# Two quads' inverse norms finished on VectorE, and a reordered opening, in a cosine-attention and feed-forward kernel

## The chip, the cores and the metric

The kernel runs on one core of a Trainium2 chip. The metric is the device time of one execution in microseconds (us); several runs are taken and the median is used. A profiled execution gives a trace: each instruction of each engine with its start, its duration and what ended the wait ahead of it. The engines are PE (matrix products), PEld (PE's weight loads, which overlap them), ACT (activation functions), DVE (elementwise work, reductions, copies), POOL (elementwise work, and a DMA queue of its own) and SP (a DMA queue).

## What is computed

```python
def _attn_ref(q, k, v, tau):                     # (8, 12, 448, 64)
    q_n = q / (np.linalg.norm(q, axis=-1, keepdims=True) + 1e-06)
    k_n = k / (np.linalg.norm(k, axis=-1, keepdims=True) + 1e-06)
    scores = np.matmul(q_n, k_n.transpose(0, 1, 3, 2)) / tau
...
    attn = np.exp(scores)                        # less the row's largest
    attn = attn / (np.sum(attn, axis=-1, keepdims=True) + 1e-09)
    return np.matmul(attn, v).astype(np.float32)

def _moe_ref(x, w_in, w_out):                    # (3584, 768), (768, 2048), (2048, 768)
    h = x @ w_in
    g = h * np.cos(h)
    return (g @ w_out).astype(np.float32)
```

The attention output, with its heads side by side, is the x of the second part.

## The kernel before

Work is cut into 24 "quads", numbered from 0. A quad is four heads of one batch row, three quads to a row. A quad's 448 keys are seven blocks of 64, so the score steps are numbered g = 7 * quad + j. A step's scores go to one of two pairs of PSUM banks (0 and 1, or 2 and 3), ACT takes their exponential into a tile E (one of 17), and PE uses E twice: in `attend` (E times V, into banks X and Y, 4 and 5) and in a sum over the keys. At the end of a quad, the AV product is multiplied by the inverse of the sums into xT, the input of the second part.

Before that, each quad is normalized. `square` takes squares of Qf and Kf, DVE adds them up into n2 (line 445), `inverse` (lines 452 to 470) turns n2 into 1 / (norm + 1e-6) by four ACT instructions, Ln, Exp, Ln, Exp, each waiting for the one before, and `scale` (472) writes Qn and Kn. Then Qn and Kn are transposed to qT and kT.

The first three quads (FIRST = 3) are the opening, lines 782 to 842. Their order on ACT, DVE and POOL is the order in which the program states them (`P.strict`), as it is on PE in the whole kernel. In the opening the transposes are PE matmuls against an identity (`transpose`, 493) with a DVE copy out of PSUM, the sums are `spread` (563, matmuls against ones, into banks 6 and 7, called Z) followed by Ln and Exp of the sums on ACT into ar (581, 582), and `scale_x` (585) multiplies banks X and Y by ar on DVE. `stir` (590) adds products with zeros to Z and `warm` (737) multiplies the identity with itself; both only keep PE occupied.

After the opening comes, for each batch row: `m1` (x times W1, then h cos h by two ACT and two DVE instructions for each pair of blocks, lines 642 to 668), `m2` (g times W2, 670 to 691, evicted by DVE copies to osb at line 684), and the scores of the next quads between the m2 parts. Quads 3 and later are scaled on POOL and transposed by DMAs from SP's queue (`turn`, 512). The normalization of quads 3 and 4 (lines 845 and 848) waits for the last ACT instruction of the opening.

Loads: Q and K of a quad are two DMAs of 448 KB on SP's queue (`load_one`), V and the weights are DMAs on POOL's queue. The load of quad 5's Q and K (line 799, `load_qk(qd + 4, half[2])`) waits for the first two of the four W2 loads.

The order on ACT, DVE, POOL and SP behind the opening, and on SP everywhere, comes from the planner (lines 22 to 195). It plays the program through with costs written at each instruction, for DMAs with a model of two queues that slow each other (`land`, 70 to 81). On each engine it takes the instruction that can start first (line 157), unless another one that can start while that one would run is more urgent by more than its lateness, its cost and WORTH = 1.0 us (line 161); urgency is counted back from PE's program order. The emitted queues run in that order whatever the chip does.

```python
c = min(pending[e], key=lambda i: (max(now, ready_at[i]), ops[i].prio))
...
if su < s + ops[c].dur and ops[c].prio - ops[u].prio > su - s + ops[u].dur + self.WORTH:
```

Of the kernel before, what the change touches and what calls it, by code (L numbers as in the profile page):

```python
# [21 lines left out]
class Planner:  # L22
# [10 lines left out]
    FIRST, LAST = 1.2, 0.8  # L33
# [9 lines left out]
    def op(self, eng, dur, fn, r=(), w=(), after=(), dma=None, moves=0, mode="f", chain=None, keep=False, lead=0.0):  # L43
        o = Op()
        o.i, o.eng, o.dur, o.fn, o.dma, o.moves, o.mode, o.chain = (
            len(self.ops), eng, dur, fn, dma, moves, mode, chain)
        o.lat = self.FIRST + moves + self.LAST if dma else self.LAT[eng]
        o.behind, o.lead = None, lead
        if keep or self.strict and eng in ("act", "dve", "pool"):
            o.behind, self.tail[eng] = self.tail.get(eng), o  # L50
        o.reads, o.writes = tuple(r), tuple(w)
        deps = {a.i for a in after if a is not None}
        for x in o.reads:
            if x in self.last_write:
# [12 lines left out]
        self.ops.append(o)  # L67
        return o
# [203 lines left out]
def bass_cosine_attention__then__act_gcu_kernel(  # L272
# [12 lines left out]
    NJ = S // D  # L285
# [6 lines left out]
    FIRST = 3  # L292
# [5 lines left out]
    def sb(name, shape, dt):  # L298
        return ctx.enter_context(nc.sbuf_tensor(name, shape, dt))

    def ring(name, n, shape, dt):
        return [sb("%s%d" % (name, i), shape, dt) for i in range(n)]

    NE, NV, NA = 17, 4, 4
# [6 lines left out]
    sqq = sb("sqq", [128, 2 * NJ, D], BF16)  # L311
    sqk = sb("sqk", [128, 2 * NJ, D], BF16)
    n2 = ring("n2", 2, [128, 4 * NJ], F32)
    nrm = ring("nrm", 2, [128, 4 * NJ], F32)
    rr = ring("rr", 2, [128, 4 * NJ], F32)
    Qn = ring("Qn", 2, [128, NJ, 2, D], BF16)
    Kn = ring("Kn", 2, [128, NJ, 2, D], BF16)
# [10 lines left out]
    ident = sb("ident", [128, 128], BF16)  # L328
    sel = sb("sel", [128, 32], BF16)
    ones = sb("ones", [128, D], BF16)  # L330
    zeros = sb("zeros", [128, 128], BF16)
    PS = ctx.enter_context(nc.psum_tensor("PS", [128, 8 * 512], F32))
    rscr = nc.dram_tensor("rscr", [2 * B * 8, S], F32)

    def bank(i, n=S, p0=0, p1=128):
        return PS.ap()[p0:p1, 512 * i:512 * i + n]
# [5 lines left out]
    op = P.op  # L342
# [11 lines left out]
    op("dve", 0.3, fill_sel, w=["sel"])  # L354
    op("dve", 0.1, lambda e: e.memset(ones.ap(), 1.0), w=["ones"])

    op("dve", 0.1, lambda e: e.memset(zeros.ap(), 0.0), w=["zeros"])

    mode = [None]

# [8 lines left out]
    def act(m, dur, fn, r=(), w=(), **kw):  # L369
        table(m)  # L370
        return op("act", dur, fn, r=[*r, "table"], w=w, **kw)
# [6 lines left out]
    def cut(kind, u, part):  # L378

        return [(kind, u, i) for i, (j0, j1) in enumerate(HALVES) if part[0] < j1 and j0 < part[1]]  # L380
# [39 lines left out]
        return pool_dma(0.79, lambda e: e.dma_start(W2.ap()[:, 4 * i:4 * i + 4, :], src),  # L420
                 w=[("W2", i)], dma=("W2", i), moves=4.32, after=after)

    H, NLEAD = 2 * NJ, 5.0

    def jr(t, w, part, off=0):
        return bass.AP(t, off + w * H + part[0], [[2 * H, 128], [NJ, 2], [1, part[1] - part[0]]])
# [24 lines left out]

    def inverse(qd, w0, w1, part=ALL[0], after=()):

        u = qd % 2
        ws = range(w0, w1)
        x = [c for w in ws for c in cut("nrm%d" % w, u, part)]
        y = [c for w in ws for c in cut("rr%d" % w, u, part)]
        if part == ALL[0]:
            n = slice(H * w0, H * w1)
            t, z, o = n2[u].ap()[:, n], nrm[u].ap()[:, n], rr[u].ap()[:, n]  # L460
        else:
            t, z, o = (jr(a[u], w0, part) for a in (n2, nrm, rr))
        act("exp", 0.12, lambda e: e.activation(z, t, ACT.Ln, bias=1e-30, scale=1.0),
            r=[c for w in ws for c in cut("n2%d" % w, u, part)], w=x, after=after, lead=NLEAD * (qd > FIRST + 1))
        yield
        act("exp", 0.12, lambda e: e.activation(z, z, ACT.Exp, bias=0.0, scale=0.5), r=x, w=x, lead=NLEAD * (qd > FIRST + 1))
        yield
        act("exp", 0.12, lambda e: e.activation(z, z, ACT.Ln, bias=1e-6, scale=1.0), r=x, w=x, lead=NLEAD * (qd > FIRST + 1))
        yield
        act("exp", 0.12, lambda e: e.activation(o, z, ACT.Exp, bias=0.0, scale=-1.0), r=x, w=y, lead=NLEAD * (qd > FIRST + 1))  # L470

    def scale(qd, w, eng="pool", part=ALL[0]):
        s, u = qd % 3, qd % 2
# [50 lines left out]
    def scores(g):  # L524
        qd, j = divmod(g, NJ)
        assert holds.get(g % NE, 0) // NJ in summed or g < NE
        holds[g % NE] = g
        u, bs, es = qd % 2, 2 * (g % 2), g % NE

        def mm(e):  # L530
            for r in range(2):
                for a in range(2):
                    ins = e.matmul(bank(bs + r, S, 64 * a, 64 * a + 64),  # L533
                                   kT[u].ap()[64 * r:64 * r + 64, j, a, :],
                                   qT[u].ap()[64 * r:64 * r + 64, :, a, :],
                                   start=True, stop=True)
# [48 lines left out]
    def scale_x(qd):  # L585
        b, c0, s = qd // QB, 2 * (qd % QB), qd % 3
        op("dve", 1.01, lambda e: e.tensor_tensor(xT[b % 2].ap()[:, c0:c0 + 2, :], two(X), ar[s].ap(), ALU.mult),
           r=pair(X) + [("ar", s)], w=[("x", b % 2, qd % QB)])

    def stir(qd, n):  # L590

        g = NJ * qd

        def mm(e):
            for i in range(n):
                ins = e.matmul(bank(Z + i % 2), zeros.ap(), E[g % NE].ap()[:, i % 2, :], start=False, stop=False)
            return ins

        op("pe", 0.19 * n, mm, r=[("E", g % NE), "zeros"], w=pair(Z), mode="q")
# [182 lines left out]
    for qd in range(FIRST):  # L782
        g = NJ * qd
        for j in range(NJ):
            scores(g + j)
            if j == 1 and qd:
                spread(qd - 1, NJ - 2, NJ - 1)
                for i in range(2):
                    attend(g - NJ + i)
                stir(qd - 1, 1)  # L790
            if j == 1 and qd == 0:
                adds[1]()
                transpose(0, 1, 7, HALVES[1])
                warm(5, X)
            if j == 2 and qd == 0:
                warm(7, X)
            if j == min(qd, 1) + 1 and qd + 1 < FIRST:
                scaled = norm_b(qd + 1, "dve")
                load_qk(qd + 4, half[2] if qd else ())
            if j == 2 and qd:  # L800
                attend(g - NJ + 2)
                spread(qd - 1, NJ - 1, NJ)
            if j == 3 and qd:
                for i in range(3, NJ):
                    attend(g - NJ + i)
                load_v(qd - 1 + NV)
                scale_x(qd - 1)
                if qd + 1 == FIRST:
                    for x in squares:
                        x()  # L810
            if j == 2:
                squares = [square(qd + 2, w, "pool", after=[scaled]) for w in range(2)]
                if qd == 0:
                    load_v(3)
                    half[2] += [load_w2(f, ()) for f in range(2)]
                    half[3] += [load_w2(f, ()) for f in range(2, 4)]
            if j == (4 if qd else 3):
                spread(qd, 0, 2)
                stir(qd, 3)
            if j == 4:  # L820
                spread(qd, 2, 3)
                if qd == 0:
                    stir(qd, 2)
            if j == 5 and qd:
                stir(qd, 1)
            if j == 5 and qd + 1 < FIRST:
                transpose(qd + 1, 0, X)
            if j == 6:
                if qd + 1 < FIRST:
                    transpose(qd + 1, 1, Y)  # L830
                    for x in squares:
                        x()
                spread(qd, 3, 5)
                stir(qd, 1)
    for i in range(4):
        attend(g + i)
    spread(qd, NJ - 2, NJ - 1)
    for i in range(4, NJ):
        attend(g + i)
    load_v(qd + NV)  # L840
    spread(qd, NJ - 1, NJ)
    scale_x(qd)
    P.strict = False
    ended = [o for o in P.ops if o.eng == "act"]
# [107 lines left out]
```

## Time and profile before

| what | value |
|---|---|
| median of 3 runs | 447.37 us (446.12 to 447.99) |
| the profiled execution | 445.76 us, of which the span from first to last instruction is 444.0 us |
| PE busy | 421.2 us, 95% of the span |
| ACT busy | 315.2 us, 71% |
| DVE busy | 249.3 us, 56% |
| POOL busy | 209.1 us, 47% |
| PE busy in the opening, 0 to 36.4 us | 7.46 of 10.7, 6.77 of 7.3, 7.66 of 9.1, 8.60 of 9.3 us |
| PE busy behind it, 101 to 365 us | 258.8 of 264 us |

PE's busy time counts matmuls that overlap, with modelled ends, so a share near 100% says that PE hardly waits, not that it runs at its peak. The last row is the sum of five stages of the trace.

### The profile page before, as it was taken

The numbers are of one execution on the slowest core, as the hardware profiler recorded it, in microseconds if no ns is written. First come the engines' busy times: TensorE is split into PE (matmuls) and PEld (weight loads), VectorE is DVE, ScalarE is ACT, GpSimd is POOL, SyncE is SP. The second block draws the span as 40 slices with busy tenths as digits, with TensorE's granted clock in tenths as the row PEclk, the third lists the DMA queues.
The fourth block names the chain that finished last, engine by engine and source line by source line (L and its number), as shares of the span: only waits on it lengthen the run. The fifth ranks groups of instructions, "written<-read, shape, count | busy, mean of one in ns | idle before, by whom it ended". The sixth has DMA issues, their size and how long they took to land.

```text
span 444.0 us, 8347 instructions
## 1 busy us (share of the span) xinstructions
PE 421.2 (95%) x3527; PEld 205.2 (46%) x3527; DVE 249.3 (56%) x278; ACT 315.2 (71%) x449; POOL 209.1 (47%) x144
## 2 busy tenths in 40 slices
PE   7889978889999999989999999999999999999996
PEld 6334433334544345434454444434454445555553
DVE  5664963446873449723984239823583136825931
ACT  6998778897778767888678656878678666815700
POOL 4675159779169792478365564188033030030000
PEclk9999999999999999999999999999999999999999
DMA  8999996998618996169923795068801611051022
GB/s 272 253 235 210 180 300 135 211 260 183 188 52 181 261 210 193 35 139 250 218 71 79 197 215 174 1 159 186 180 2 36 161 39 38 0 156 35 1 71 71
DMA packets 70589, 64.79 MB, mean 146 GB/s; under 512 B 41924, under 2 KB 62744, under 8 KB 70552
## 3 DMA queue, kind: packets, MB, share of 16 engines
q1 hardware_dynamic: 60144, 52.31, 47.3%
q0 software_dynamic: 10240, 11.80, 16.4%
q8 instruction: 27, 0.44, 0.4%
q10 hardware_dynamic: 168, 0.15, 0.1%
q14 instruction: 10, 0.08, 0.1%
HBM read 55.25 MB, written 11.16 MB: 150 GB/s over the span
## 4 chain that ended last, share of the span: by engine, by line
PE 64%; ACT 11%; DMA 9%; POOL 6%; DVE 5%; issue 2%; SPq 1%; ACTq 1%; POOLq 0%
PE PS L648 25%; PE PS L676 24%; ACT E L540 8%; PE PS L533 6%; PE PS L550 4%; DMA Qf<-in_q_dram 3%; PE PS L615 3%; DMA Kf<-in_k_dram 3%; DMA kT<-Kn 2%; DVE n L445 1%; POOL xT L634 1%; POOL sqq L441 1%; POOL Kn L478 1%; POOL Qn L478 1%; POOL sqk L441 1%
## 5 line engine op out<-in xcount | busy, mean ns | idle before, releaser
L540 ACT ACTIVATE E<-PS 128x896 bf16<-128x896 f32 x168 | 145.3, 916 | 33.1 <-PE PS L533 28.4
L676 PE MATMUL PS<-W,gT 128*128 128x384 bf16 x896 | 163.4, 327 | 3.5 <-DVE osb L684 2.6
L648 PE MATMUL PS<-xT,W 128*128 128x448 bf16 x768 | 148.2, 353 | 0.9 <-DVE gT L667 0.8
L676 PEld LDWEIGHTS PS<-W,gT 128*128 128x128 bf16 x896 | 80.1, 98 | 83.9 <-issue 28.8
L648 PEld LDWEIGHTS PS<-xT,W 128*128 128x128 bf16 x768 | 74.1, 98 | 72.2 <-DVE gT L667 2.2
L661 ACT ACTIVATE ar<-PS 128x896 int32<-128x896 f32 x64 | 58.1, 910 | 45.6 <-PE PS L648 45.2
L663 DVE SCALAR_TENSOR_TENSOR ar<-ar,PS 128x896 f32<-128x896 int32 x64 | 69.0, 1083 | 26.3 <-ACT ar L661 26.3
L684 DVE COPY osb<-PS 128x384 f32<-128x384 f32 x56 | 30.3, 556 | 94.6 <-PE PS L676 94.6
L634 POOL TENSOR_TENSOR xT<-AVs,R 128x896 bf16<-128x896 f32 x21 | 43.6, 2085 | 71.5 <-DMA R<-rscr 71.3
L665 ACT ACTIVATE ar<-ar 128x896 f32<-128x896 f32 x64 | 60.6, 947 | 14.7 <-DVE ar L663 14.4
L667 DVE TENSOR_TENSOR gT<-PS,ar 128x896 bf16<-128x896 f32 x64 | 69.4, 1088 | 1.5 <-ACT ar L665 1.0
L533 PE MATMUL PS<-qT,kT 64*64 64x448 bf16 x672 | 55.3, 366 | 9.9 <-ACT E L540 7.6
L441 POOL TENSOR_TENSOR sqq<-Qf 128x896 bf16<-128x896 f32 x22 | 36.9, 1676 | 57.0 <-DVE n L445 26.6
L550 PE MATMUL PS<-E,Vb 64*64 64x448 bf16 x672 | 48.0, 351 | 0.3 <-DVE AVs L559 0.2
L478 POOL TENSOR_TENSOR Qn<-Qf,rr 128x896 bf16<-128x896 f32 x21 | 35.4, 1688 | 27.1 <-ACT rr L470 27.1
L441 POOL TENSOR_TENSOR sqk<-Kf 128x896 bf16<-128x896 f32 x22 | 36.9, 1677 | 21.5 <-DVE n L445 14.5
L559 DVE COPY AVs<-PS 128x896 f32<-128x896 f32 x21 | 22.9, 1090 | 27.2 <-PE PS L550 27.1
L533 PEld LDWEIGHTS PS<-qT,kT 64*64 64x64 bf16 x672 | 15.3, 104 | 45.9 <-ACT E L540 25.6
L445 DVE TENSOR_REDUCE n<-sqq 128x14 f32<-128x896 bf16 x24 | 25.9, 1081 | 17.1 <-POOL sqq L441 11.8
L478 POOL TENSOR_TENSOR Kn<-Kf,rr 128x896 bf16<-128x896 f32 x21 | 35.5, 1689 | 0.0
L445 DVE TENSOR_REDUCE n<-sqk 128x14 f32<-128x896 bf16 (+2 forms) x25 | 26.0, 1043 | 12.8 <-POOL sqk L441 12.7
L550 PEld LDWEIGHTS PS<-E,Vb 64*64 64x64 bf16 x672 | 19.5, 106 | 11.9 <-issue 2.4
(43 smaller groups left out, 163.2 us busy)
## 6 DMA issues: line engine op xcount, KB each, us to landing
Qf<-in_q_dram SPq DMA_DIRECT2D x24, 448.0 KB, 4.7
out_dram<-osb SPq DMA_DIRECT2D x56, 192.0 KB, 2.8
Kf<-in_k_dram SPq DMA_DIRECT2D x23, 448.0 KB, 5.7
R<-rscr SPq DMA_DIRECT2D x42, 224.0 KB, 4.5
Vb<-in_v_dram POOLq DMA_DIRECT2D x24, 224.0 KB, 7.0
W<-in_moe_w_in_dram POOLq DMA_DIRECT2D x4, 768.0 KB, 18.4
W<-in_moe_w_out_dram POOLq DMA_DIRECT2D x4, 768.0 KB, 24.9
qT<-Qn SPq DMA_TRANSPOSE x21, 4.6
```

The lines of the kernel that those rows point to most:

```text
L441: op(eng, (1.68 if eng == "pool" else 1.05) * n, lambda e: e.tensor_tensor(dst, src, src, ALU.mult), r=cut(nm + "f", s, part), w=cut("sq" ...
L445: return op("dve", 0.07 + 0.95 * n, lambda e: e.tensor_reduce(out=n2[u].ap()[:, H * w:H * w + H] if part == ALL[0] else jr(n2[u], w, part) ...
L478: lambda e: e.tensor_tensor(n[u].ap()[:, j0:j1].rearrange("p j r d -> p r j d"), f[s].ap()[:, :, j0:j1], rb, ALU.mult),
L533: ins = e.matmul(bank(bs + r, S, 64 * a, 64 * a + 64), kT[u].ap()[64 * r:64 * r + 64, j, a, :], qT[u].ap()[64 * r:64 * r + 64, :, a, :], s ...
L540: act("exp", 0.875, lambda e: e.activation(E[es].ap(), two(bs), ACT.Exp, bias=0.0, scale=INV_TAU), r=pair(bs), w=[("E", es)], chain="E")
L550: ins = e.matmul(bank((X, Y)[a], S, 64 * r, 64 * r + 64), Vb[vs].ap()[64 * a:64 * a + 64, r, j, :], E[es].ap()[64 * a:64 * a + 64, r, :], ...
L648: ins = e.matmul(bank(bk + i2), W1.ap()[:, i, 128 * nb:128 * nb + 128], xT[c % 2].ap()[:, i, :], start=(i == 0), stop=(i == NKC - 1))
L661: op("act", 0.815, lambda e: e.activation(ar[s].ap().bitcast(I32), two(bk), ACT.Identity, bias=0.25, scale=INV2PI), r=bs, w=[("ar", s)])
L663: op("dve", 1.005, lambda e: e.scalar_tensor_tensor(ar[s].ap(), ar[s].ap().bitcast(I32), -2.0 * math.pi, two(bk), ALU.mult, ALU.add), r=bs ...
L665: act("sin", 0.86, lambda e: e.activation(ar[s].ap(), ar[s].ap(), ACT.Sin, bias=GUARD * math.pi / 2.0, scale=GUARD), r=[("ar", s)], w=[("a ...
L667: op("dve", 1.01, lambda e: e.tensor_tensor(gT.ap()[:, 2 * pr:2 * pr + 2, col:col + S], two(bk), ar[s].ap(), ALU.mult), r=bs + [("ar", s)] ...
L676: ins = e.matmul(bank(bk, HW), gT.ap()[:, f, col:col + 128], W2.ap()[:, f, HW * h:HW * h + HW], start=(f == 0), stop=(f == NNB - 1))
```

## The change

Five things change; the names are those of the code.

1. `inverse` of quads 1 and 2 keeps Ln and Exp on ACT, which leave the norms. nrm becomes a tile of pairs: Exp writes one of a pair, the other holds 1e-6 from the start (`fill_eps`). A DVE reduction adds each pair, a DVE reciprocal follows. Quad 0 and quads 3 and later keep the four ACT instructions, on the wider nrm.
2. Quad 2 is transposed into Z and Z + 1 (banks 6 and 7) instead of X and Y. Quad 1's first sums, which used Z at that time, move to steps 0 and 1 of quad 2; quad 1's three `stir` calls of its own pass go, and `warm(8, Z)` stands ahead of the transposes. `scale_x(0)` moves behind the copies of those transposes.
3. In quad 0, the last two `spread` products are split around the transposes of quad 1, with one more `stir` product.
4. At the end of the opening the last `spread` stands ahead of the last three `attend` steps instead of behind them.
5. `zeros` shares the memory of `iot`, which is filled again once the identity is made.

```diff
-    nrm = ring("nrm", 2, [128, 4 * NJ], F32)
+    nrm = ring("nrm", 2, [128, 4 * NJ, 2], F32)
...
-    zeros = sb("zeros", [128, 128], BF16)
+    zeros = iot.ap().bitcast(BF16)[:, 0:128]
...
+    def fill_eps(e):
+        e.memset(nrm[0].ap(), 1e-6)
+        return e.memset(nrm[1].ap(), 1e-6)
...
+        if 0 < qd <= FAST:
+            op("dve", 0.13, lambda e: e.tensor_reduce(out=o, in_=both, axis=AX.X, op=ALU.add), r=cells("nrm") + ["eps"],
+               w=cells("rr"), lead=lead)
+            yield
+            op("dve", 0.27, lambda e: e.reciprocal(o, o), r=cells("rr"), w=cells("rr"), lead=lead)
+            return
...
             scores(g + j)
+            if j < 2 and qd == 2:
+                spread(qd - 1, 3 * j, 3 * j + 3 - j)
...
-                scale_x(qd - 1)
                 if qd + 1 == FIRST:
+                    scale_x(qd - 1)
...
-            if j == (4 if qd else 3):
+            if j == (4 if qd else 3) and qd != 1:
                 spread(qd, 0, 2)
                 stir(qd, 3)
             if j == 4:
-                spread(qd, 2, 3)
+                if qd == 1:
+                    warm(8, Z)
+                    transpose(qd + 1, 0, Z)
+                else:
+                    spread(qd, 2, 3)
...
-            if j == 5 and qd:
-                stir(qd, 1)
-            if j == 5 and qd + 1 < FIRST:
-                transpose(qd + 1, 0, X)
+            if j == 5:
+                if qd == 0:
+                    transpose(qd + 1, 0, X)
+                    spread(qd, 3, 4)
+                elif qd == 1:
+                    transpose(qd + 1, 1, Z + 1)
+                    scale_x(qd - 1)
+                else:
+                    stir(qd, 1)
...
-    for i in range(4):
+    for i in range(3):
         attend(g + i)
     spread(qd, NJ - 2, NJ - 1)
+    attend(g + 3)
+    spread(qd, NJ - 1, NJ)
     for i in range(4, NJ):
         attend(g + i)
     load_v(qd + NV)
-    spread(qd, NJ - 1, NJ)
     scale_x(qd)
```

More of the change, by code (lines that the diff above doesn't have):

```diff
@@ L355, in bass_cosine_attention__then__act_gcu_kernel @@
     op("dve", 0.1, lambda e: e.memset(ones.ap(), 1.0), w=["ones"])
-    op("dve", 0.1, lambda e: e.memset(zeros.ap(), 0.0), w=["zeros"])
+    op("dve", 0.1, lambda e: e.memset(zeros, 0.0), w=["zeros", "iot"])
+    def fill_eps(e):
+        e.memset(nrm[0].ap(), 1e-6)
+        return e.memset(nrm[1].ap(), 1e-6)
+    op("dve", 0.2, fill_eps, w=["eps"] + [(n, u, i) for n in ("nrm0", "nrm1") for u in range(2) for i in range(3)])
     mode = [None]
@@ L421, in load_w2 @@
                  w=[("W2", i)], dma=("W2", i), moves=4.32, after=after)
-    H, NLEAD = 2 * NJ, 5.0
+    H, NLEAD, FAST = 2 * NJ, 5.0, 2
     def jr(t, w, part, off=0):
@@ L455, in inverse, with cells @@
         ws = range(w0, w1)
-        x = [c for w in ws for c in cut("nrm%d" % w, u, part)]
-        y = [c for w in ws for c in cut("rr%d" % w, u, part)]
+        def cells(name):
+            return [c for w in ws for c in cut("%s%d" % (name, w), u, part)]
+        j0, j1 = part
+        rows = [NJ, 2 * (w1 - w0)], [1, j1 - j0]
         if part == ALL[0]:
[L459 to L462, printed above, removed]
@@ L463, in inverse @@
-        act("exp", 0.12, lambda e: e.activation(z, t, ACT.Ln, bias=1e-30, scale=1.0),
-            r=[c for w in ws for c in cut("n2%d" % w, u, part)], w=x, after=after, lead=NLEAD * (qd > FIRST + 1))
+            rows = [[1, H * (w1 - w0)]]
+        t, o = (bass.AP(x[u], w0 * H + j0, [[2 * H, 128], *rows]) for x in (n2, rr))
+        wide = [[2 * a, b] for a, b in rows]
+        z = bass.AP(nrm[u], 2 * (w0 * H + j0), [[4 * H, 128], *wide])
+        both = bass.AP(nrm[u], 2 * (w0 * H + j0), [[4 * H, 128], *wide, [1, 2]])
@@ L465, in inverse @@
+        lead = NLEAD * (qd > FIRST + 1)
+        act("exp", 0.12, lambda e: e.activation(z, t, ACT.Ln, bias=1e-30, scale=1.0), r=cells("n2"), w=cells("nrm"),
+            after=after, lead=lead)
         yield
-        act("exp", 0.12, lambda e: e.activation(z, z, ACT.Exp, bias=0.0, scale=0.5), r=x, w=x, lead=NLEAD * (qd > FIRST + 1))
+        act("exp", 0.12, lambda e: e.activation(z, z, ACT.Exp, bias=0.0, scale=0.5), r=cells("nrm"), w=cells("nrm"), lead=lead)
         yield
-        act("exp", 0.12, lambda e: e.activation(z, z, ACT.Ln, bias=1e-6, scale=1.0), r=x, w=x, lead=NLEAD * (qd > FIRST + 1))
+        if 0 < qd <= FAST:
[4 more added lines that the diff above has]
+            return
@@ L469, in inverse @@
+        act("exp", 0.12, lambda e: e.activation(z, z, ACT.Ln, bias=1e-6, scale=1.0), r=cells("nrm"), w=cells("nrm"), lead=lead)
         yield
-        act("exp", 0.12, lambda e: e.activation(o, z, ACT.Exp, bias=0.0, scale=-1.0), r=x, w=y, lead=NLEAD * (qd > FIRST + 1))
+        act("exp", 0.12, lambda e: e.activation(o, z, ACT.Exp, bias=0.0, scale=-1.0), r=cells("nrm"), w=cells("rr"), lead=lead)
     def scale(qd, w, eng="pool", part=ALL[0]):
@@ L595, in mm @@
             for i in range(n):
-                ins = e.matmul(bank(Z + i % 2), zeros.ap(), E[g % NE].ap()[:, i % 2, :], start=False, stop=False)
+                ins = e.matmul(bank(Z + i % 2), zeros, E[g % NE].ap()[:, i % 2, :], start=False, stop=False)
             return ins
@@ L820, in bass_cosine_attention__then__act_gcu_kernel @@
             if j == 4:
-                spread(qd, 2, 3)
+                if qd == 1:
[3 more added lines that the diff above has]
+                    spread(qd, 2, 3)
                 if qd == 0:
                     stir(qd, 2)
-            if j == 5 and qd:
-                stir(qd, 1)
-            if j == 5 and qd + 1 < FIRST:
-                transpose(qd + 1, 0, X)
-            if j == 6:
+            if j == 5:
[7 more added lines that the diff above has]
+                    stir(qd, 1)
+            if j == 6:
+                if qd == 0:
+                    transpose(qd + 1, 1, Y)
+                    spread(qd, 4, 5)
+                    stir(qd, 2)
+                elif qd == 2:
+                    spread(qd, 3, 5)
+                    stir(qd, 1)
                 if qd + 1 < FIRST:
-                    transpose(qd + 1, 1, Y)
                     for x in squares:
                         x()
-                spread(qd, 3, 5)
-                stir(qd, 1)
-    for i in range(4):
+    for i in range(3):
         attend(g + i)
     spread(qd, NJ - 2, NJ - 1)
+    attend(g + 3)
+    spread(qd, NJ - 1, NJ)
     for i in range(4, NJ):
```

## The prediction

> **What bounds the kernel now.** I read the busy time by stage first: behind 101 us PE is busy 258.8 of 264 us, so whatever shift arrives there goes through to the end, and whatever the change is worth is decided ahead of it. Next the chain that ended last, in order of time (start, us, what), where it leaves the opening:
>
> ```profile
> 37.45 0.96 ACT ar L582
> ...
> 39.52 1.68 POOL Qn L478
> 41.20 1.65 POOL Kn L478
> 42.85 1.65 POOL Qn L478
> 44.49 1.66 POOL Kn L478
> 46.15 2.27 SPq L517
> ...
> 48.54 11.07 DMA Qf<-in_q_dram
> ...
> 59.68 1.68 POOL sqq L441
> 61.36 1.65 POOL sqk L441
> ...
> 63.03 1.10 DVE n L445
> ...
> 64.15 0.23 ACT nrm L463
> ```
>
> The chain does not run through m1, which fills PE from 36.4 to 55 us. It runs through a load that takes 11.07 us: Q of quad 5. Its squares are added by DVE at 63.03, and what stands behind that addition is shown by the timelines of DVE and PE:
>
> ```profile
> 63.03 1.09 DVE L445 TENSOR_REDUCE n<-sqk 128x14 f32<-128x896 bf16 x1 [0.55 <-POOL sqk L441]
> 64.03 1.01 DVE L684 COPY osb<-PS 128x384 f32<-128x384 f32 x2
> 64.64 0.82 PE L676 MATMUL PS<-W,gT 128*128 128x384 bf16 x4 [1.65 <-DVE osb L684]
> ```
>
> The eviction, and PE behind it, wait for quad 5's squares; ACT's exponentials (idle 1.98 us ahead of 64.15) stand behind its Ln. Why the load is slow, the SP timeline and the DMA queues say (30 to 41, 44 to 50, 58 to 62 us):
>
> ```profile
> 42.87 5.55 SPq L517 DMA_TRANSPOSE kT<-Kn  x1
> 48.54 0.51 SPq L393 DMA_DIRECT2D Qf<-in_q_dram  x1
> 49.10 0.49 SPq L393 DMA_DIRECT2D Kf<-in_k_dram  x1
> 49.64 7.07 SPq L517 DMA_TRANSPOSE qT<-Qn  x1
> 56.74 3.29 SPq L517 DMA_TRANSPOSE kT<-Kn  x1
> ```
>
> ```profile
> q0 software_dynamic: 1526, 2.28, 114.9%
> ...
> q0 software_dynamic: 716, 1.08, 98.0%
> q1 hardware_dynamic: 557, 0.14, 17.8%
> ...
> q1 hardware_dynamic: 2345, 1.28, 115.8%
> ```
>
> The DMA engines are full from 30 us on with POOL's weights (q0). SP's queue (q1) gets 557 packets in 6 us beside them, 93 per us, and 2345 in 4 us, 586 per us, once they are through. Four transposes are 3840 of the packets under 512 bytes between 41 and 63 us, 960 each.
>
> **The change part by part.**
> Quad 1's norms: on ACT, 12.72 (Ln) to 13.63 (next exponential) is 0.91 us, four steps 0.26 apart with the last overlapped. Two steps are 0.26 + 0.13 = 0.39: ACT gains 0.52. DVE gets two instructions that no row shows. The sum of 56 elements: the additions of 896 take 1.08 us, two of 512 and 384 together 1.14, a slope near 1.05 ns per element and some 0.14 fixed, so 0.2. The reciprocal of 28: from 0.07 (a memset here) to 1.08 (896 elements); it is nearest to the small ones, and I take 0.3. Qn then starts at 13.21 + 0.03 + 0.2 + 0.03 + 0.3 + 0.03 = 13.80 against 13.76, and PE's transposes (15.89) do not wait for that; with 1.08 Kn would be 0.8 late, and quad 2's Qn with it. [...]
>
> With exponentials 0.52 earlier, PE's order decides: step 4's scores 14.06, stir to 15.1, step 5's scores, transpose to 15.9, one spread, step 6's scores, second transpose 16.4 to 16.95, DVE copy to 17.6. Scores of quad 1 start at 17.65 against 17.99: -0.35.
>
> Quad 2's norms: 20.83 to 21.75 becomes 0.39, again -0.53, but n2 is ready at 20.4 and ACT now arrives at 20.45; nothing more is to be had there. The sums' Ln starts at 20.85 instead of 21.75 and ends at 21.75, and PE, which waits 1.17 us for it before, goes on with warm (8 at 0.09) and the transposes. Qn is ready at 22.5, Kn at 23.6, copies of both at 25.1. Scores of quad 2 start at 25.2 instead of 27.13 and ACT has no gap any more (before 0.69 at 27.57): -1.7 at its first exponential. Five spread products, 0.95 us of PE, now stand in steps 0 and 1 of quad 2 and cost ACT some 0.5 at its third exponential; the later steps give the same order as before. I get -1.3 at the sums' Ln (30.10 to 28.8).
>
> Last sums first: the exponential of step 20 ends near 33.9, the last spread at 34.45, ahead of three attends of 0.19 = 0.57. Ln of the sums starts at 34.5 against 36.50: **-2.0**; scale_x and the norms of quads 3 and 4 follow it (38.43 to 36.4). PE, though, has 0.57 of attend and 2.75 of m1 first, so its second m1 part starts at 37.8 against 39.57: **-1.75**. Both of the fills (zeros, eps) are memsets of 0.1 in a DVE idle from 1.5 to 5.29, so nothing; without that cover they are 0.3.
>
> **What becomes of 1.75 us.** m1 is PE and DVE work alone; W2 lands at 50.9 at the latest, and m2 comes to 54.25. But PE then meets line 684, and quad 5's load does not follow the engines. SP's queue could start its transposes 2.0 us earlier, which at 93 packets per us is 186 packets, 0.3 us at the later rate. With SP's order as it is, Q lands near 59.3 and the wait of 1.65 grows to some 3.1.
>
> The order will not stay. Quad 5's load waits for the second W2 load, which lands at 42.4 in the trace and is issued at 20.7 from POOL, ahead of anything that moves. Quad 4's transposes wait for POOL's Qn and Kn, which move by 2.0. In the planner's own books for the kernel before (worked from its costs; only an order is taken from them, no time) the transposes of quad 4 are ready at 45.16 and 46.81 and the load at 45.43; the load goes first because it is 1.85 more urgent, just over the 0.27 + 0.5 + 1.0 that line 161 asks. Moved by 1.96 in the same books, the transposes are ready at 43.20 and 44.85, the load stays, and line 161 asks 0.58 + 1.5 = 2.08 for the second one. So both transposes go **ahead of the load**, with a margin of 0.23.
>
> Then SP issues 39.2 (qT), 40.9 to 46.5 (kT, 5.55), to 53.6 (7.07) and to 56.9 (3.29), or 57.9 if the full queue holds it by packets; the load follows with 4.8 us to landing (the row of quad 7, 62.37) or 3.9 (quad 6, 60.14): 60.8 to 62.7. By work done: all of this was through at 62.3 before, and the two loads are now last, so K lands near 62.5. I take Q at 61.8, 2.2 after 59.6. POOL's squares, DVE's additions, the eviction and ACT's Ln all follow in order: PE goes on at 66.8 instead of 64.64, **+2.2** (bounds +1.2 and +3.1), while it came there at 61.2 instead of 62.99.
>
> The sum on the profiled execution: 444.0 + 2.2 = 446.2 span, 447.96 with the 1.76 around it. Its 445.76 stands 1.61 under the median of the runs, so **449.6** beside 447.37. This case alone: 448.5 to 450.5.
>
> **Rivals.**
> *PE's clock falls in the longer stall.* PE stands from 61.2 to 66.8, 5.6 us; the longest stall behind the opening was 1.65. Nothing in the trace shows a slower clock (granted 1.00 all through), but the first 40 identity products, after idle, take 4.18 us, 104 ns each, the next 24 take 73, the next 5 take 56. That beginning costs 40 x 48 + 24 x 17 ns = 2.3 us. In the scores' stage PE is busy 16.59 of 20 us, and the 17% of slack takes a part: from 0 to 2.3, I take 1.4, which gives 451.0. [...]
>
> *The transfer is hidden anyway.* The order flips only for qT (+0.8, since Q waits for 960 packets more) or not at all (-0.3): 447.1 to 448.2, no change. For it speaks the margin of 0.23.
>
> *The other side: the whole gain arrives.* If quad 5's load is issued behind the first transposes at 46.5 and lands by 57.9, which takes a queue that follows its issue time, every later step moves by 1.75: 445.6. It decides at the landing of quad 5's K: at or below 59.0 this case holds. The full queue from 30 to 56 us speaks against it.
>
> *The change does not shorten the opening* (the reciprocal takes 1.08): quad 2's transposes come 0.8 later, the gain at 39 us falls to 1.0, and SP's order flips for qT alone: in the second case's times.
>
> **Chances.** Forecast 0.38 (449.6), clock 0.24 (451.0), no change 0.25 (447.1 to 448.2), whole gain 0.13 (445.6). About 0.5%, 2.2 us, is what a measurement of this kernel can tell from no change: slower means above 449.6, which is half of the forecast and nearly all of the clock case, 0.19 + 0.23 and a remainder of 0.03: 0.45. Faster means below 445.1: less than half of the last case and reorderings that I cannot see, 0.11. The rest, 0.44, is no change. The range 445.5 to 451.7 leaves out half of the last case and the longest stalls.
>
> **What would show it.** Right: Ln of the last sums near 34.5, quads 3 and 4 scaled on POOL from 37.5; SP issuing four transposes in a row and quad 5's Q behind them near 57; POOL's first square near 62; a PE wait on DVE osb of 5 us or more; equal stages from 101 us on. Clock: m2 products behind that wait at double their 190 ns. Wrong: Q of quad 5 ahead of quad 4's transposes on SP, or the eviction ahead of quad 5's additions on DVE with ACT's Ln late in its queue, which would let PE keep its 1.75.

## The result and the profile after

The changed kernel takes 453.56 us (median of 4 runs, 450.69 to 455.02) beside 446.75 us for the kernel before, measured with it: ratio 1.0139 [1.0098, 1.0180], slower. Measured again on two chips it gave 1.0099 [1.0064, 1.0134] and 1.0075 [1.0046, 1.0103]; the three, weighed by the inverse squares of their half widths, give 1.0097 [1.0077, 1.0116], some 4.3 us. The profiled execution has a span of 452.9 us (before 444.0).

In the opening the new work costs what it was priced at. DVE's timeline, then ACT's (start us, duration us, engine, line, operation, tiles, idle before and what ended it):

```profile
13.24 0.21 DVE L483 TENSOR_REDUCE rr<-nrm 128x28 f32<-128x56 f32 x1 [0.38 <-ACT nrm L480]
13.49 0.33 DVE L486 RECIPROCAL rr<-rr 128x28 f32<-128x28 f32 x1
13.85 1.09 DVE L498 TENSOR_TENSOR Qn<-Qf,rr 128x896 bf16<-128x896 f32 x1
...
35.03 0.92 ACT L601 ACTIVATE ar<-PS 128x896 f32<-128x896 f32 x1 [0.81 <-PE PS L592]
```

The Ln of the last sums comes at 35.03 instead of 36.50. Then SP, whose order has turned (its timeline from 39 us):

```profile
39.77 1.33 SPq L537 DMA_TRANSPOSE qT<-Qn  x1
41.42 5.97 SPq L537 DMA_TRANSPOSE kT<-Kn  x1
47.44 6.14 SPq L537 DMA_TRANSPOSE qT<-Qn  x1
53.62 4.16 SPq L537 DMA_TRANSPOSE kT<-Kn  x1
57.90 0.51 SPq L399 DMA_DIRECT2D Qf<-in_q_dram  x1
58.46 0.46 SPq L399 DMA_DIRECT2D Kf<-in_k_dram  x1
```

Four transposes go in a row and quad 5's load follows at 57.90, where it went behind the first two at 48.54 before. What waits for it, on all engines:

```profile
61.79 1.68 POOL L447 TENSOR_TENSOR sqq<-Qf 128x896 bf16<-128x896 f32 x1 [17.10 <-DMA Qf<-in_q_dram]
65.14 1.09 DVE L451 TENSOR_REDUCE n<-sqk 128x14 f32<-128x896 bf16 x1 [0.55 <-POOL sqk L447]
66.14 1.01 DVE L704 COPY osb<-PS 128x384 f32<-128x384 f32 x2
66.26 0.23 ACT L477 ACTIVATE nrm<-n 128x28 f32<-128x28 f32 x1 [5.21 <-DVE n L451]
66.75 1.46 PE L696 MATMUL PS<-W,gT 128*128 128x384 bf16 x4 [4.88 <-DVE osb L704]
69.78 1.46 PE L696 MATMUL PS<-W,gT 128*128 128x384 bf16 x4
72.32 0.82 PE L696 MATMUL PS<-W,gT 128*128 128x384 bf16 x4
```

It is the chain of before, squares to additions to eviction to m2, 2.1 us later, and PE stands for 4.88 us. The four products behind the wait take 1.46 us, and so do the next four; 0.82 comes back only at 72.3. The stretches of 2 us say why (busy us and instructions of PE, PEld, DVE, ACT, POOL, then the granted clock, the DMA share, GB/s):

```profile
64.00:66.00 2.00, 0.00 (x0) 0.00 (x0) 1.45 (x2) 0.00 (x0) 1.11 (x1) 0.83 1.04 376
66.00:68.00 2.00, 1.25 (x4) 0.44 (x4) 1.16 (x3) 1.74 (x4) 0.00 (x0) 0.50 0.59 217
68.00:70.00 2.00, 2.00 (x18) 0.76 (x18) 0.00 (x0) 1.55 (x5) 0.11 (x1) 0.50 0.76 197
70.00:72.00 2.00, 2.00 (x16) 0.67 (x14) 0.00 (x0) 0.81 (x2) 2.00 (x2) 0.50 0.00 0
72.00:74.00 2.00, 2.00 (x28) 0.72 (x22) 0.11 (x1) 1.23 (x2) 2.00 (x2) 0.97 0.53 103
```

The granted clock is 0.50 from 66 to 72 us. And a second stall stands where none was forecast, at m1 of row 1 (timelines of all engines):

```profile
93.00 0.57 ACTq L645 DMA_DIRECT2D rscr<-Zs  x1
93.44 1.48 POOL L411 DMA_DIRECT2D Vb<-in_v_dram  x2
98.52 3.36 SPq L651 DMA_DIRECT2D R<-rscr  x4
103.20 2.07 POOL L654 TENSOR_TENSOR xT<-AVs,R 128x896 bf16<-128x896 f32 x1 [1.91 <-DMA R<-rscr]
105.33 1.69 PE L668 MATMUL PS<-xT,W 128*128 128x448 bf16 x8 [0.67 <-POOL xT L654]
107.31 2.07 POOL L654 TENSOR_TENSOR xT<-AVs,R 128x896 bf16<-128x896 f32 x1 [2.03 <-DMA R<-rscr]
109.43 4.88 PE L668 MATMUL PS<-xT,W 128*128 128x448 bf16 x16 [2.41 <-POOL xT L654]
```

The sums of row 1 go through DRAM: written at 93.00, read back from 98.52, 5.52 us later. Two loads of V are issued on POOL in that time. Before, the same write was issued at 89.30 and the reads at 92.80, 3.50 us later, with one load of V between them, and PE did not wait:

```profile
89.30 0.58 ACTq L625 DMA_DIRECT2D rscr<-Zs  x1
90.15 0.76 POOL L405 DMA_DIRECT2D Vb<-in_v_dram  x1
92.80 2.39 SPq L631 DMA_DIRECT2D R<-rscr  x4
...
100.80 4.70 PE L648 MATMUL PS<-xT,W 128*128 128x448 bf16 x24
```

PE's first product of each point, against before (us, one profile each; m2[32] is the first behind the wait for the eviction, m1[96] the first of row 1):

| point | before | after | load first | flip alone | filled | old order, flip | V late | V early | told order |
|---|---|---|---|---|---|---|---|---|---|
| m1[16] | 39.58 | -1.07 | -1.07 | -0.09 | -1.11 | -0.67 | -0.97 | -1.10 | -1.01 |
| m2[24] | 60.52 | -1.12 | -1.34 | -0.10 | -1.38 | -0.65 | -1.25 | -1.38 | -1.28 |
| m2[32] | 64.64 | +2.11 | +0.49 | +2.88 | +1.94 | +2.72 | +1.36 | +2.11 | -1.81 |
| m2[60] | 78.96 | +4.68 | +1.64 | +4.72 | +2.62 | +3.53 | +3.19 | +4.49 | +0.98 |
| m2[92] | 99.14 | +3.70 | +1.05 | +4.27 | +1.64 | +3.09 | +2.53 | +7.72 | +0.33 |
| m1[96] | 100.80 | +4.53 | +1.74 | +4.27 | +2.76 | +3.09 | +3.59 | +7.72 | +0.45 |
| m1[120] | 105.75 | +8.82 | +2.27 | +4.59 | +4.58 | +3.62 | +7.53 | +7.72 | +0.99 |
| last m2 | 439.34 | +8.94 | +3.00 | +4.34 | +4.76 | +3.33 | +7.66 | +8.73 | +1.00 |

From m1[120] on the shift moves by about a microsecond at most: it is made by then. "After" is the longest of the three profiles of the changed kernel. The second ("the changed kernel again" below) is at +2.04 at m2[32], +4.16 at m2[60], +3.54 at m1[96], +5.14 at m1[120] and +5.01 at the end, the third (beside the runs on the second stall) at +2.63, +4.28, +3.29, +3.78 and +3.76.

### The profile page after: what moved, and what is told of

Its sections match the earlier page's. It is cut to its first block, busy times and chain, and to the rows that moved or that the text cites. A ratio compares the mean times of both kernels' runs of the same rounds, so it can differ in the third digit from the quotient of the medians.

```text
span 452.9 us, 8356 instructions
## 1 busy us (share of the span) xinstructions
PE 424.3 (94%) x3531; PEld 206.7 (46%) x3531; DVE 250.5 (55%) x284; ACT 315.3 (70%) x445; POOL 209.3 (46%) x144
## 4 chain that ended last, share of the span: by engine, by line
PE 66%; ACT 10%; DMA 8%; POOL 5%; DVE 4%; SPq 4%; issue 1%; ACTq 0%
PE PS L668 26%; PE PS L696 25%; ACT E L560 7%; PE PS L553 6%; PE PS L570 4%; PE PS L635 3%; SPq L537 3%; DMA Qf<-in_q_dram 3%; DMA R<-rscr 2%; DMA rscr<-Zs 2%; DVE n L451 1%; POOL sqq L447 1%; POOL Kn L498 1%; POOL Qn L498 1%; DMA Kf<-in_k_dram 1%
## 5 line engine op out<-in xcount | busy, mean ns | idle before, releaser
L668 PE MATMUL PS<-xT,W 128*128 128x448 bf16 x768 | 149.8, 355 | 3.6 <-POOL xT L654 3.1
L570 PE MATMUL PS<-E,Vb 64*64 64x448 bf16 x672 | 49.0, 355 | 0.8 <-DVE AVs L579 0.5
L447 POOL TENSOR_TENSOR sqk<-Kf 128x896 bf16<-128x896 f32 x22 | 36.9, 1677 | 19.3 <-DVE n L451 12.7
```

The lines of the kernel that those rows point to most:

```text
L447: op(eng, (1.68 if eng == "pool" else 1.05) * n, lambda e: e.tensor_tensor(dst, src, src, ALU.mult), r=cut(nm + "f", s, part), w=cut("sq" ...
L570: ins = e.matmul(bank((X, Y)[a], S, 64 * r, 64 * r + 64), Vb[vs].ap()[64 * a:64 * a + 64, r, j, :], E[es].ap()[64 * a:64 * a + 64, r, :], ...
L668: ins = e.matmul(bank(bk + i2), W1.ap()[:, i, 128 * nb:128 * nb + 128], xT[c % 2].ap()[:, i, :], start=(i == 0), stop=(i == NKC - 1))
```

## The experiments

### The load first again

In the changed kernel, the load's gate is the first W2 load alone:

```diff
-                load_qk(qd + 4, half[2] if qd else ())
+                load_qk(qd + 4, half[2][:1] if qd else ())
```

> The changed kernel, with quad 5's load waiting for the first W2 load alone instead of the first two; that puts the load back ahead of quad 4's transposes in SP's order, as before the change, and leaves ACT's order behind the opening as it was before. Theory 1 (the loss comes from SP's order): the load is issued near 47.4 us, behind quad 3's two transposes, and lands near 59.3; PE's wait for the eviction falls from 4.9 us to about 2.5 to 3; the time is 445 to 448 us, within 0.5% of before. Rival (the loss sits in the new opening itself, its banks or its DVE work, or in the clock whatever the order): the time stays above 450 us.

448.49 us, ratio 1.0011 [0.9976, 1.0046]. Quad 5's load is ahead of quad 4's transposes again (SP, POOL and PE of this run):

```profile
47.45 0.66 SPq L399 DMA_DIRECT2D Qf<-in_q_dram  x1
48.14 0.49 SPq L399 DMA_DIRECT2D Kf<-in_k_dram  x1
48.67 8.53 SPq L537 DMA_TRANSPOSE qT<-Qn  x1
...
60.17 1.68 POOL L447 TENSOR_TENSOR sqq<-Qf 128x896 bf16<-128x896 f32 x1 [15.49 <-DMA Qf<-in_q_dram]
...
65.13 0.88 PE L696 MATMUL PS<-W,gT 128*128 128x384 bf16 x4 [3.48 <-DVE osb L704]
```

The loss is gone, so the turn of SP's order starts it. But the opening's gain doesn't arrive: issued 1.09 us earlier than before, Q is squared 0.49 us later.

### The turn alone, in the kernel before

```diff
-                load_qk(qd + 4, half[2] if qd else ())
+                load_qk(qd + 4, half[2] + half[3][:1] if qd else ())
```

> The kernel before, with nothing of the change, but quad 5's load waiting for the third W2 load as well (landed at 46.5 us in the trace, so it holds nothing up by itself); this alone turns SP's order to four transposes in a row and then the load, and leaves the order on ACT, DVE and POOL as it was. Theory 1: the load is issued near 60 us and lands near 64, PE waits for the eviction from 63 to about 69 (5.9 us), matmuls behind that wait take twice as long for some 3 to 5 us, and the time is 450 to 454 us, as slow as the change or nearly so. Rival (opening): within 0.5% of before.

450.05 us, 1.0063 [1.0027, 1.0099]. The opening is that of before and only the load goes later (58.56): a wait of 4.63 us for the eviction, products of 1.46 us per four behind it, and no stall for xT. The turn and its stall cost 0.6% without anything else of the change.

### The stall filled

```diff
         flush_av()
+        if steps[0] == 23:
+            def mm(e):
+                for i in range(24):
+                    ins = e.matmul(bank(X + i % 2), zeros, E[4].ap()[:, i % 2, :], start=False, stop=False)
+                return ins
+            op("pe", 0.0, mm, r=[("E", 4), "zeros"], w=pair(X), mode="q")
```

> The changed kernel with 24 products with zeros (some 4.6 us of PE) added to banks X and Y ahead of the m2 that waits for the eviction; they change no value, and the planner is told a cost of zero, so that every queue keeps its order. Theory 2 (the long stall also costs PE's clock): the four m2 products behind the wait take 0.82 us instead of 1.46, PE reaches the sums near 72.4 instead of 73.8, and the time falls by about 1.4 us against the changed kernel, to about 452. Rival (the slow products are contention, not the clock): they stay at 1.46 us and the time stays at 453.5.

451.76 us, 1.0092 [1.0057, 1.0126]. PE's timeline in it:

```profile
61.54 4.71 PE L750 MATMUL PS<-E,iot 128*128 128x448 bf16 x24
66.58 0.82 PE L696 MATMUL PS<-W,gT 128*128 128x384 bf16 x4 [0.33 <-DVE osb L704]
68.79 0.82 PE L696 MATMUL PS<-W,gT 128*128 128x384 bf16 x4
```

With PE busy in the wait, the products behind it keep 0.82 and the granted clock is 1.00 throughout. In the traces the way from m2[32] to m2[60] takes 0.68 us longer than before (2.62 - 1.94) instead of 2.57 in the changed kernel, so the slow clock is worth 1.9 us of that execution. The ratio, though, isn't clearly under those of the changed kernel, and the wait for xT came all the same (2.6 us): the run time doesn't show the clock's price by itself.

### No gate on the load

```diff
-                load_qk(qd + 4, half[2] if qd else ())
+                load_qk(qd + 4)
```

> The changed kernel with quad 5's load waiting for no W2 load: it goes out near 23 us, as soon as quad 2's scaling has freed the buffer, and competes with the W2 loads, which land some 4 us later (near 55 at the latest, still ahead of the m2 that needs them near 58). Theory 1: POOL squares quad 5 within m1, no wait for the eviction is left behind 61 us, and the 1.75 us of the opening plus the 1.65 of the old wait arrive: 442 to 445 us. Rival (W2 or DVE's additions within m1 become the bound): 446 to 449 us.

453.22 us, 1.0111 [1.0076, 1.0145]: a miss. The load does what was expected: it goes out at 22.94, quad 5's Q is squared at 33.19 instead of 59.68, and no wait for the eviction over 0.3 us is left. But without the gate the planner reordered ACT, DVE, POOL and SP, and other waits take the place of that one: 1.94 us for a transposed K at 60.66, which lands 18.3 us after its issue (15.6 before), 1.87 us for an exponential at 75.72, and 2.21 us for a copy by DVE at 101.17. Behind each of them the granted clock is 0.50 for about 3.4 us. An early load thus takes the first stall away, but this run can't say what that is worth.

### The planner told that the load is late

```diff
-            o.end = self.land(e, avail[e], o.moves) if o.dma else s + o.dur + o.lat
+            o.end = self.land(e, avail[e], o.moves) + o.late if o.dma else s + o.dur + o.lat
...
+                for o in load_qk(qd + 4, half[2] if qd else ()):
+                    o.late = 7.0 * qd
```

In the kernel before, with 7.0 us:

> The kernel before, with one thing told to its planner: quad 5's loads land 7 us later than its own model says (the trace has them 6 to 7 later). SP's and POOL's orders stay; DVE's first eviction moves ahead of quad 5's second addition, and ACT takes two more exponentials ahead of quad 5's first Ln. Theory (what sets the time near 62 us is the queueing of other work behind a load that comes late, not the load itself): PE's wait of 1.65 us for the eviction falls below 0.3 and the time falls by 1 to 1.7 us, to 0.996 to 0.998 of before. Rival (the wait only moves, to quad 5's transposes near 78 us): 0.999 to 1.002.

445.48 us, 0.9969 [0.9937, 1.0000]. Knowing of the late landing, the planner puts the eviction between quad 5's two additions and two exponentials ahead of its Ln; m2 goes on at 62.88, and PE waits 0.3 us at most for an eviction. In the changed kernel, with 9.0 us and the gate on one W2 load:

> The changed kernel with quad 5's load back ahead of quad 4's transposes (as in the first experiment) and its planner told that the load lands 9 us later than its model says; the evictions then stand ahead of quad 5's additions on DVE, and quad 5's Ln behind four more exponentials on ACT. Theory: PE goes on near 61.5 us instead of 65.1, without a stall that costs its clock, and the 1.1 to 1.3 us of the opening arrive together with the old wait: 443.5 to 445 us, 0.992 to 0.996 of before. Rival (quad 5's normalization is now late and PE waits for its transposes near 75 to 78 us): 446 to 448 us.

446.49 us, 0.9976 [0.9945, 1.0006]. The same remedy takes all of the loss away, but the opening's gain is again not seen. (Its profiled execution is 3 us late already at m1[16], since the granted clock is halved for 6.8 us between 10 and 20 us, and isn't read in points. It has the second stall too: two loads of V beside a write of 5.44 us, and 1.8 us of waiting for xT.)

### The turn, with the old order behind it

Each queue of the changed kernel is given the order that the planner chose for "the turn alone":

```diff
+    ORDER = {"act": act_ranks, "dve": dve_ranks, "pool": pool_ranks, "sp": sp_ranks}
+    for e, ranks in ORDER.items():
+        mine = [o for o in P.ops if o.eng == e]
...
+        for k in ranks:
+            mine[k].behind = before
+            before = mine[k]
     P.emit(nc, ctx)
```

> The changed kernel, each queue behind the opening in the order that the second experiment (the flip alone) had, so that quad 5's load still goes out behind four transposes, but the order further on is that of the kernel before. Theory 3 (the second stall near 105 us, xT waiting for R, comes from the new order of loads and stores further on, not from the flip): m1 of the second batch row waits less than 1 us for xT, and the time is 1.003 to 1.009 of before. Rival (whatever is late by 4 us at 76 us meets the same stall): the wait for xT stays at 2 to 3 us and the ratio at 1.012 to 1.016.

450.25 us, 1.0062 [1.0034, 1.0089]. The wait for the eviction is there (5.01 us), the wait for xT is 0.34. So in this profile the second stall goes with the order of the queues behind the opening, not with the turn. The clock in its stretches of 2 us:

```profile
66.00:68.00 2.00, 0.64 (x3) 0.30 (x4) 2.00 (x4) 1.12 (x4) 2.00 (x2) 0.73 0.92 330
68.00:70.00 2.00, 2.00 (x19) 0.76 (x17) 1.73 (x2) 1.55 (x4) 1.00 (x1) 0.50 0.47 103
70.00:72.00 2.00, 2.00 (x25) 0.69 (x18) 0.12 (x1) 1.65 (x4) 1.49 (x1) 0.92 0.29 94
```

The half clock lasts half as long here as in the changed kernel's profile (3.4 us against 6.8), after as long a stall (5.01 us against 4.88), and m2[32] to m2[60] takes 0.81 us more than before.

### The last sums first, alone

The kernel before with the reordering of the last attends and spreads, and nothing else:

```diff
-    for i in range(4):
+    for i in range(3):
         attend(g + i)
     spread(qd, NJ - 2, NJ - 1)
+    attend(g + 3)
+    spread(qd, NJ - 1, NJ)
...
-    spread(qd, NJ - 1, NJ)
```

> The kernel before with the last part of the change alone, the last sums ahead of the last three AV steps. Theory: the norms of quads 3 and 4 come 0.5 to 0.6 us earlier, which turns SP's order for the first of quad 4's transposes only; quad 5's load is issued near 53 us and lands near 60.4, 0.8 later, and the time is 1.000 to 1.004 of before. Rival (a shorter opening is a gain unless both transposes pass the load): 0.998 to 1.000.

447.85 us, 1.0013 [0.9981, 1.0045]. No difference that shows: quad 5's load (54.04) goes between quad 4's transposes, Q is squared at 60.40, and PE waits 1.74 us for the eviction. That is only 0.09 more than before, yet the granted clock behind it is 0.88, 0.50 and 0.76 from 64 to 70 us, where before it stays at 1.00.

### The changed kernel again

> The changed kernel as it is, once more and on another chip, to see whether both stalls come back and to have its ratio from more runs. Theory (flip, stall and slow clock, then a second stall for xT by the new order behind the opening): ratio 1.010 to 1.016; PE waits 4.5 to 5.2 us for the eviction near 66.5 us and 2.5 to 3.5 us in sum for xT of row 1 behind 100 us; products of the second part of m2 at half rate behind the first wait. Rival (one profile caught an accident): one of the two waits is under 1 us, ratio 1.005 or less.

452.00 us, 1.0099 [1.0064, 1.0134]. Both stalls are there: 4.96 us for the eviction, 0.20 + 1.43 for xT; the write of row 1's sums takes 5.01 us (92.48 to 97.49).

### The changed opening in the order of before

The same forced order, with the ranks of the kernel before.

> The changed kernel's opening, but every queue behind the opening in the order of the kernel before, so quad 5's load stays ahead of quad 4's transposes and nothing is reordered later. Theory (the new order alone is what costs; the load itself is bound by the full DMA engines and gains nothing from an earlier opening): Q of quad 5 lands and is squared at 59.3 to 60.3, PE waits 2.8 to 3.8 us for the eviction, m2 behind it at +0.0 to +0.7, xT wait under 1 us, ratio 0.998 to 1.003. Rival (the opening costs by itself, as by slower transfers or a slower clock): ratio 1.005 or more. Rival (the gain of 1.1 us arrives when the order is kept): m2 behind the wait at -0.8 or less, ratio 0.997.

448.69 us, 1.0026 [0.9994, 1.0058]. Q is squared at 59.80 as expected, but the wait for the eviction is 2.02 us only, since this execution reached m1[16] no earlier than before (+0.02), which leaves it open what an early m1 would have gained there. The clock is halved behind 2.02 us too: granted 0.79, 0.50, 0.86 from 64 to 70 us.

### The turn, the old order and the stall filled

The 24 products of zeros in the forced order of the turn.

> The run with the forced older order (load behind the transposes, no xT stall), with 24 products of zeros added on PE in the long wait for the eviction, so that PE does not stand idle there. Theory (the slow clock behind the wait is worth 1.3 to 2 us of the 2.7 us lost there): PE at full rate behind the wait, the end 1.2 to 2 us ahead of the run without them, ratio 1.002 to 1.004 against 1.0062. Rival (the scores' slack swallows the slow products): the same end within 0.5 us, ratio 1.005 to 1.007.

452.09 us, 1.0083 [1.0048, 1.0118]: a miss. The products keep 0.82 us per four and m2[32] to m2[60] takes no longer than before, but the time is no shorter than without them. The profiled execution (457.72 us) met 1.62 us of waiting for a transposed K at 60.5 and a loss of 6 us behind 226 us that no other profile shows and that isn't explained here. The traces price the clock at 0.8 us against the run without the products; the run times don't bear it out.

### The changed opening in the told order

The forced order again, with the ranks that the planner chose for the kernel before when told of the landing.

> A candidate to beat both: the changed kernel's opening with every queue behind it in the order that the planner gave the kernel before when it was told that quad 5's load lands late (the eviction and the exponentials go ahead of quad 5's additions and norms; that order alone measured 0.9969). Theory (with the eviction no longer behind quad 5's squares, PE keeps its 1.07 us of the opening): no PE wait over 1.2 us for the eviction, m2 behind it at -2.5 or less, ratio 0.992 to 0.996. Rival (the next late thing is quad 5's own scores or its loads, which do not move with the opening): ratio 0.996 to 0.999, no better than that order without the change.

447.27 us, 1.0001 [0.9969, 1.0033]: the candidate doesn't beat that order without the change. POOL, DVE, PE and ACT in it:

```profile
59.51 1.68 POOL L447 TENSOR_TENSOR sqq<-Qf 128x896 bf16<-128x896 f32 x1 [14.76 <-DMA Qf<-in_q_dram]
...
62.22 1.01 DVE L704 COPY osb<-PS 128x384 f32<-128x384 f32 x2
...
62.83 0.82 PE L696 MATMUL PS<-W,gT 128*128 128x384 bf16 x4 [1.12 <-DVE osb L704]
...
64.26 0.23 ACT L477 ACTIVATE nrm<-n 128x28 f32<-128x28 f32 x1 [1.46 <-DVE n L451]
```

PE is 1.81 us ahead at m2[32], yet ACT's Ln stands at 64.26, against 64.15 in the kernel before and 64.08 in the told one, and has now waited 1.46 us. Everything ahead of quad 5's norms came earlier, and the norms did not. Nor is the lead of 1.81 us the opening's: the told kernel without the change is 1.76 us ahead at m2[32] (62.88). In both, the eviction stands behind quad 5's first addition (61.22 here, 61.04 there), and the opening's microsecond is gone in the wait for it. At m2[60] the told kernel is at -0.49, this one at +0.98. Both wait 1.56 us for an exponential at 74.0; behind it the granted clock is 0.82, 0.50 and 0.83 here from 74 to 80 us, and 1.00 there.

### Which operation makes the second stall

Between the two orders, two loads of V on POOL stand out: in the changed kernel they come some 10 us later (89.39 and 93.44 us, against 80.48 and 82.88 in the forced older order), into the round trip of row 1's sums. One run moves only these two ahead in the changed kernel's own order (its diff below), one only these two back in the forced older order; the third is the changed kernel beside them.

```diff
     "pool": [
...
-        -107, -103, -102, -101, -104, -100, -99, -98, -93,
+        -107, -104, -98, -103, -102, -101, -100, -99, -93,
...
```

> The changed kernel with every queue in its own order, but two of POOL's loads of V put 3 and 5 places further ahead, where the run with the forced older order has them. Theory (the V loads fill the DMA engines while row 1's sums go through DRAM, and that makes the second stall): the write of the sums takes 3.4 to 4.2 us instead of 5.0 to 5.5, PE waits under 1.2 us in sum for xT of row 1, the products of row 1 and all behind them come 1 to 3 us earlier than in the changed kernel, ratio 1.005 to 1.009. The first stall near 66 us stays (4.5 to 5.2 us). Rival (SP's transposes and loads, or the moved vector work, make it): the wait for xT stays at 1.5 us or more and the ratio at 1.010 or more.

454.49 us, 1.0115 [1.0076, 1.0154]: the stall goes, the time stays (SP, POOL, PE, ACT):

```profile
83.37 1.47 POOL L411 DMA_DIRECT2D Vb<-in_v_dram  x2
83.46 1.51 SPq L537 DMA_TRANSPOSE kT<-Kn  x1
...
91.95 0.75 PE L553 MATMUL PS<-qT,kT 64*64 64x448 bf16 x8 [2.51 <-DMA kT<-Kn]
...
97.03 0.57 ACTq L645 DMA_DIRECT2D rscr<-Zs  x1
...
99.52 0.47 SPq L651 DMA_DIRECT2D R<-rscr  x1
```

The write of the sums takes 2.49 us and PE doesn't wait for xT. But the two loads now go out beside the transposes of a K, which land 8.4 us after their issue instead of 4.3 in the changed kernel, and PE waits 2.51 us for them, with the clock at 0.66 behind it (92 to 97 us).

> The reverse: the forced older order (1.0062, xT wait 0.34 us) with the same two loads of V moved 5 and 4 places back, where the changed kernel has them, and nothing else. Theory (V loads make the second stall): the write of row 1's sums takes 4.5 us or more instead of 3.6, PE waits 1 to 3 us for xT of row 1, ratio 1.008 to 1.014. Rival: the wait stays under 0.7 us and the ratio at 1.005 to 1.007.

452.49 us, 1.0095 [1.0065, 1.0125], against 1.0062 [1.0034, 1.0089] without the move on another chip; the intervals overlap. The trace is plain (timelines of POOL, ACT, SP, PE):

```profile
91.60 1.48 POOL L411 DMA_DIRECT2D Vb<-in_v_dram  x2
91.84 0.57 ACTq L645 DMA_DIRECT2D rscr<-Zs  x1
...
97.32 2.39 SPq L651 DMA_DIRECT2D R<-rscr  x4
...
104.39 1.69 PE L668 MATMUL PS<-xT,W 128*128 128x448 bf16 x8 [0.89 <-POOL xT L654]
...
108.15 4.88 PE L668 MATMUL PS<-xT,W 128*128 128x448 bf16 x16 [2.07 <-POOL xT L654]
```

The write takes 5.48 us instead of 3.57, PE waits 2.96 us for xT instead of 0.34, and m1[120] is at +7.53 instead of +3.62. In these traces, one of each kernel, two loads of V, moved alone, make the second stall.

> The changed kernel as it is, on the same chip as the two before. Theory: ratio 1.010 to 1.014, both stalls there again (4.5 to 5.2 us for the eviction near 66 us; 1.4 to 3.3 us in sum for xT of row 1). Rival: the second one is absent in this profile, so that it is not a matter of the order alone.

452.38 us, 1.0075 [1.0046, 1.0103]. The first stall is there (4.79 us); the write of the sums takes 4.62 us, and the wait for xT is only 0.31. So the stall differs between executions of one kernel, with the time that the write takes: over the three profiles of the changed kernel a write of 5.52, 5.01 and 4.62 us left PE waiting 3.08, 1.63 and 0.31 us, in the order of the three ratios.

## Why the prediction was right and wrong

**The sign and the mechanism were right up to 66.8 us.** SP's four transposes in a row (forecast 39.2, 40.9, 46.5, 53.6; measured 39.77, 41.42, 47.44, 53.62), the load behind them, Q at 61.8 (61.79), PE going on at 66.8 (66.75): each within 1 us. That some agree to 0.02 us is luck: the transposes started 0.57 us later than forecast, and the third then held SP for 6.14 us instead of 7.07. The order that the planner's books gave by a margin of 0.23 came. The forecast as a ratio is 449.6 / 447.37 = 1.0050; the runs that hold the forecast's mechanism and the slow products behind it, the turn alone and the turn with the old order, measured 1.0063 and 1.0062.

**The opening's gain was mis-sized.** Pair sum and reciprocal are 0.21 and 0.33 (0.2 and 0.3 forecast), but quad 1's scores came 0.14 earlier instead of 0.35, the last sums' Ln 1.47 instead of 2.0, and the second m1 part 1.07 instead of 1.75. It changed the length of the stall (4.88 instead of 5.6), not its end, which the load sets.

**The clock was a rival and should have been a term.** The forecast kept full speed behind a stall of 5.6 us, since no row of before showed another. The slow products (1.46 us per four instead of 0.82) came in every profile with that stall unless PE was kept busy in it: 1.83 to 2.57 us more from m2[32] to m2[60] in the five profiles with 6.8 us at half clock, 0.81 and 1.65 in the two with 3.4, against 0.68 and 0.00 in the two filled runs. The 1.4 us of the rival was of the right size in the traces (by the two filled runs, 0.8 to 1.9). In the run times it isn't shown: neither filled kernel was faster.

**The step that failed carries the shift at 66.8 us to the end.** The forecast took its +2.2 at the eviction for +2.2 at the end, with "equal stages from 101 us on", and so put everything behind the stall at nothing. In the profile the shift is +2.11 there, as forecast, but +4.68 at m2[60], by the slow products, +3.70 at m2[92], and +8.82 at m1[120]; the two other profiles end at +5.01 and +3.76. The tail is bound by PE (busy 250.7 of 256 us from 118 to 374 us in the changed kernel's profile), and the shift stays within about a microsecond from m1[120] on. But the forecast looked in the planner's books for the place of one load and carried everything between 66 and 101 us over in its old order. The planner also moved two loads of V by some 10 us there, into the write and reading back of row 1's sums. In the traces that made the wait for xT of 0.3 to 3.1 us and, in the worst profile, another 3.4 us at half clock (m1[104] to m1[120], +1.70): forcing the old order leaves 0.34 us of this wait, and moving the two loads alone brings it to 2.96. What it costs in time stays open. The changed kernel, 1.0097, is 0.35% above the two runs without the move, little more than the uncertainty. V early was no faster, since another wait came, and the told version of the changed kernel has 0.9976 with a wait of 1.8 us for xT in its profile.

**The rivals on the other side fell.** "The whole gain arrives" needs a load that follows its issue: issued 1.09 us earlier it was squared 0.49 us later. With the eviction put ahead of the second addition PE was 1.81 us early with the change and 1.76 without it, since the first addition waits for the same load. In both, the opening's gain ends at quad 5's Q. Of the versions run, the best are the told orders (0.9969 and 0.9976), and neither is clearly faster than the kernel before.

## What to carry to other kernels

Where a planner sets the order, a stage made shorter can reorder every queue behind it: compare the orders of all queues, loads first, up to the point where one engine bounds the rest, before carrying a shift through. A gain ahead of a transfer need not pass it: here quad 5's Q, issued 1.09 us earlier, was squared 0.49 us later, and with the eviction let past its second addition PE was 1.81 us early, but the Ln of quad 5's norms stood at 64.26 us against 64.15 before. A stall of some microseconds on PE is to be priced with the slow products behind it, as a term of the sum; here the traces give that price as 0.8 to 1.9 us, and the run times don't confirm it.

## What the runs showed of the hardware

**The half clock comes in portions.** In slices of 0.1 us of the changed kernel's profile the granted clock is 1.00 or 0.50, with other values only where it changes; it is at 0.50 from 65.3 to 72.2 us and from 109.6 to 113.1. In stretches of 2 us, time at half clock is then twice the stretch times what the granted clock lacks of 1. In the changed kernel (64 to 74 us) that is 4 x (0.17 + 0.50 + 0.50 + 0.50 + 0.03) = 6.8 us, in the run with the old order 4 x (0.27 + 0.50 + 0.08) = 3.4 us; the run with the turn alone has 6.8, the changed opening in the order of before 3.4. Over the 17 profiles, 20 such stretches end inside the program; each has 3.4 or 6.8 us, and none anything between. What makes a portion 3.4 us long is not shown here. Between 1.5 and 2.3 us, the length of PE's wait alone does not tell the clock behind it: half speed followed waits of 1.56 us (the told order), 1.74 (the last sums alone) and 2.02 (the order of before), and full speed waits of 1.56 (the told kernel), 1.65 (the kernel before), 1.79 and 2.25 (108 and 268 us in the filled run with the old order). Behind every wait from 2.41 us (109.43 us in the changed kernel) to 5.13 (V early) the clock was halved.

**A small write took longer beside two loads.** From the issue of the write to the issue of its reading back, the same 14 KB of row 1's sums took 4.6 to 5.5 us in the seven profiles with two loads of V (224 KB each) issued between 2.5 us ahead of the write and 2 us behind it, 1.9 to 4.2 in the nine with one, and 2.5 in the one with none. Quad 5's Q took 12.7 us from issue to use in the middle of the transposes and weights (47.45 to 60.17, the load first) and 3.9 behind them (57.90 to 61.79, the changed kernel).
